# The 32nd largest of two sorted lists by a scan of maxima and minima, and the softmax division moved into the next step

## The chip, the cores and the metric

The kernel runs on one core of one Trainium2 chip. The metric is the device time of one launch, in microseconds (us). The kernel before took 1684.64 us, the median of three runs (1683.96 to 1685.89). The engines are called TensorE (PE; its weight loads PEld), VectorE (DVE), ScalarE (ACT), GpSimd (POOL) and SyncE (SP, which issues the DMA transfers here).

## The reference

Top-k attention, then a two-layer network with the SmeLU activation, all in fp32:

```python
# q, k, v: (B=8, H=8, S=576, D=64)
scores = scale * np.matmul(q, k.transpose(0, 1, 3, 2))
kth = np.partition(scores, -32, axis=-1)[..., -32:-31]
scores = np.where(scores >= kth, scores, -1000000000.0)
scores = scores - np.max(scores, axis=-1, keepdims=True)
attn = np.exp(scores)
attn = attn / (np.sum(attn, axis=-1, keepdims=True) + 1e-09)
attn_out = np.matmul(attn, v)
# (B,H,S,D) -> (B*S, H*D) = (4608, 512)
h = x @ w_in                                   # (512, 2048)
g = np.where(h >= 1, h, np.where(h <= -1, 0.0, (h + 1) ** 2 / 4.0))
out = g @ w_out                                # (2048, 512)
```

Each row of 576 scores keeps its 32 largest; what is kept is normalised by its sum plus 1e-9.

## The kernel before

The attention runs in 144 steps. A step handles 128 query rows of two heads, that is a tile of 128 partitions with 2 rows of 576 scores each, `s`. VectorE has an instruction that finds the 8 largest values of a row in falling order (`max`) and one that overwrites given 8 values in a row (`match_replace`). To make the rows half as long, the 576 scores are taken in 288 pairs: `more` holds the larger of each pair, `less` the smaller. The 32 largest of `more` come from four rounds, the 8 largest of `less` from one (`seconds`), and the 32nd largest of both lists together is the threshold `kth`. If more than 8 of the smaller ones could matter, `excess` shows it and a second, plain pass (`paired` is False) runs.

```python
def first_top(st):                      # of the next step, called within this one
    s = st["s"]
    if paired:
        pairs(st)                       # more = max of the two halves of s
    st["tops"] = tops = att.tile([P, 2, TOP_K + 8], F32, name="tops", bufs=3)
    st["e"] = e = att.tile([P, 2, S], F32, name="e", bufs=3)
    nmax = att.tile([P, 2], F32, name="nmax")
    for i in range(2):
        nc.vector.max(out=tops[:, i, 0:8], in_=(st["more"] if paired else s)[:, i, :])
    nc.scalar.activation(nmax, tops[:, :, 0], AF.Copy, scale=-1.0)
    for i in range(2):
        nc.scalar.activation(e[:, i, :], s[:, i, :], AF.Exp, bias=nmax[:, i:i + 1])
        yield

def weights(st, after):
    # ...
    for r in range(8, TOP_K, 8):
        for i in range(2):
            nc.vector.match_replace(out=rest[:, i, :], in_to_replace=tops[:, i, r - 8:r],
                                    in_values=src[:, i, :], imm_value=LOWEST)
        src = rest
        if r == 8:
            yield
        if r + 8 == TOP_K:
            yield
            yield from first_top(after) if after is not None else (None, None)
        for i in range(2):
            nc.vector.max(out=tops[:, i, r:r + 8], in_=src[:, i, :])
    if paired:
        nc.vector.tensor_tensor(out=less, in0=s[:, :, 0:SH], in1=s[:, :, SH:S], op=ALU.min)
        seconds = att.tile([P, 2, 8], F32, name="seconds")
        for i in range(2):
            nc.vector.max(out=seconds[:, i, :], in_=less[:, i, :])
        nc.vector.tensor_tensor(out=tops[:, :, TOP_K:TOP_K + 8], in0=tops[:, :, TOP_K - 2:TOP_K - 10:-1],
                                in1=seconds, op=ALU.min)
        for i in range(2):
            nc.vector.max(out=kth[:, i, :], in_=tops[:, i, TOP_K - 1:TOP_K + 8])
        last = kth[:, :, 0]
    # ...
    for i in range(2):                  # masks the exponentials, and sums them into z
        nc.vector.scalar_tensor_tensor(out=e[:, i, :], in0=s[:, i, :], scalar=last[:, i:i + 1],
                                       in1=e[:, i, :], op0=ALU.is_ge, op1=ALU.mult,
                                       accum_out=z[:, i:i + 1])
    yield
    rz = att.tile([P, 2], F32, name="rz")
    nc.vector.tensor_scalar(z, z, 1e-9, None, ALU.add)
    nc.vector.reciprocal(rz, z)
    if st["by_tensor"]:                 # the first 12 steps and the last 2
        # ... ScalarE scales an identity by rz; TensorE transposes and divides with it
    else:                               # the 130 others
        for i in range(2):
            nc.gpsimd.tensor_scalar(e[:, i, :], e[:, i, :], rz[:, i:i + 1], 1.0, ALU.mult, ALU.mult)
    # ... GpSimd notes the excess
    yield
```

In the 130 later steps the weights are transposed by DMA: ScalarE splits them into 16-bit halves, they go to DRAM, and a transposing DMA brings them back as `wT`, which `values` multiplies with v on TensorE.

```python
def move_w(st):
    # ...
    for i in range(2):
        nc.scalar.copy(halves[:, :, i * S:(i + 1) * S], st["e"][:, i, :].bitcast(U16).rearrange("p (k t) -> p t k", t=2))
    # ...
    nc.sync.dma_start(out=rows, in_=halves)
    nc.sync.dma_start_transpose(wT.bitcast(U16), rows.rearrange("p t k -> (p t) k"))
```

The two-layer network works on chunks of one or two tiles of 128 tokens. `hidden` makes 128 of the 2048 hidden values on TensorE (`ph`, 128 or 256 columns), ScalarE and GpSimd apply the activation, and `final` accumulates 512 outputs (`py`) on TensorE.

All engines are in order, and the order of their instructions is fixed when the program is built: a step has 7 slots, in each of which the attention's generator advances by one part and some units of the network are put in. How many is decided by a small model of the time, in which K_TIME stands for a step's length.

```python
K_TIME, PIECE_TIME, UNIT_TIME, SLOTS, EARLY_STEPS, EARLY_SHARE = 10.2, 0.55, 0.218, 7, 4, 32
# ...
for m in range(n + 2):
    # ...
        parts = [1] * SLOTS if early else [1, 1, 0, 1, 1, 1, 1]
    # ...
    for slot in range(SLOTS):
        # ...
        for _ in range(parts[slot]):
            next(top_k, None)
        # ...
        if slot == 2 and 1 <= m <= n and not state[m - 1]["by_tensor"]:
            move_w(state[m - 1])
            ready_at[m - 1] = done[m - 1] + 14.0
        # ...
        if slot == 4:
            begin_at(m + 2)             # the scores of the step after next
        if slot == 5 and not early:
            values_until(m - 1)
        # ...
        advance((EARLY_SHARE if early else share) / SLOTS if m < n else 32.0, now)
```

Of the kernel before, what the change touches and what calls it, by code (L numbers as in the profile page):

```python
# [10 lines left out]
F32 = mybir.dt.float32  # L11
# [3 lines left out]
AF = mybir.ActivationFunctionType  # L15
# [3 lines left out]
TOP_K = 32  # L19
# [5 lines left out]
def kernel(  # L25
# [37 lines left out]
    nc.gpsimd.memset(half, 0.5)  # L63
    minus = const.tile([P, 1], F32, name="minus")
    nc.gpsimd.memset(minus, -1.0)
    two = const.tile([P, 1], F32, name="two")
    nc.gpsimd.memset(two, 2.0)

# [9 lines left out]
    for i in range(2):  # L78
        v_tails.append([const.tile([P, H, D], F32, name=f"v_tail{i}{x}") for x in range(2)])
        for x in v_tails[i]:  # L80
            nc.gpsimd.memset(x, 0.0)

# [72 lines left out]
    def run(ctx, paired):  # L157
# [99 lines left out]
        def scores(st):  # L257
            t, hp, kT, qT = st["t"], st["hp"], st["keys"]["kT"], st["qT"]
            st["s"] = s = att.tile([P, 2, S], F32, name="s", bufs=3)
            for hf in range(2):  # L260
# [9 lines left out]
                                             start=True, stop=True)  # L270
                nc.scalar.activation(s[:, :, c0:c1], sp[:, :, 0:SH], AF.Copy, scale=SCALE)  # L271

# [6 lines left out]
        def first_top(st):  # L282
            s = st["s"]
            if paired:
                pairs(st)
            st["tops"] = tops = att.tile([P, 2, TOP_K + 8], F32, name="tops", bufs=3)
            st["e"] = e = att.tile([P, 2, S], F32, name="e", bufs=3)
            nmax = att.tile([P, 2], F32, name="nmax")
            for i in range(2):
                nc.vector.max(out=tops[:, i, 0:8], in_=(st["more"] if paired else s)[:, i, :])  # L290
            nc.scalar.activation(nmax, tops[:, :, 0], AF.Copy, scale=-1.0)
            for i in range(2):
                nc.scalar.activation(e[:, i, :], s[:, i, :], AF.Exp, bias=nmax[:, i:i + 1])  # L293
                yield


        def weights(st, after):
            s, m, tops, e = st["s"], st["m"], st["tops"], st["e"]
            kth = att.tile([P, 2, 8], F32, name="kth", bufs=3)
            if paired:  # L300
                src = rest = less = st["more"]
            else:
                src, rest = s, att.tile([P, 2, S], F32, name="rest", bufs=1)
            for r in range(8, TOP_K, 8):
                for i in range(2):
                    nc.vector.match_replace(out=rest[:, i, :], in_to_replace=tops[:, i, r - 8:r],  # L306
                                            in_values=src[:, i, :], imm_value=LOWEST)
                src = rest
                if r == 8:
                    yield  # L310
                if r + 8 == TOP_K:
                    yield
                    yield from first_top(after) if after is not None else (None, None)
                for i in range(2):
                    nc.vector.max(out=tops[:, i, r:r + 8], in_=src[:, i, :])  # L315
            if paired:
                nc.vector.tensor_tensor(out=less, in0=s[:, :, 0:SH], in1=s[:, :, SH:S], op=ALU.min)  # L317
                seconds = att.tile([P, 2, 8], F32, name="seconds")
                for i in range(2):
                    nc.vector.max(out=seconds[:, i, :], in_=less[:, i, :])  # L320
                nc.vector.tensor_tensor(out=tops[:, :, TOP_K:TOP_K + 8], in0=tops[:, :, TOP_K - 2:TOP_K - 10:-1],
                                        in1=seconds, op=ALU.min)
                for i in range(2):
                    nc.vector.max(out=kth[:, i, :], in_=tops[:, i, TOP_K - 1:TOP_K + 8])  # L324
                last = kth[:, :, 0]
            else:
                last = tops[:, :, TOP_K - 1]
            z = att.tile([P, 2], F32, name="z")
            for i in range(2):
                nc.vector.scalar_tensor_tensor(out=e[:, i, :], in0=s[:, i, :], scalar=last[:, i:i + 1],  # L330
                                               in1=e[:, i, :], op0=ALU.is_ge, op1=ALU.mult,
                                               accum_out=z[:, i:i + 1])
            yield
            rz = att.tile([P, 2], F32, name="rz")
            nc.vector.tensor_scalar(z, z, 1e-9, None, ALU.add)  # L335
            nc.vector.reciprocal(rz, z)  # L336
            if st["by_tensor"]:
                st["rz"] = diag = (late or words).tile([P, 2, P], F32, name="diag", bufs=1)
                for i in range(2):
                    nc.scalar.activation(diag[:, i, :], ident, AF.Copy, scale=rz[:, i:i + 1])  # L340
            else:
                for i in range(2):
                    nc.gpsimd.tensor_scalar(e[:, i, :], e[:, i, :], rz[:, i:i + 1], 1.0, ALU.mult, ALU.mult)  # L343
            if paired:
                nc.gpsimd.tensor_tensor(out=excess[:, 2 * m:2 * m + 2], in0=seconds[:, :, 7], in1=kth[:, :, 0],
                                        op=ALU.subtract)
            yield

# [112 lines left out]
        for b in range(0, B, 2):  # L463
            a, c, tl = [(b, t) for t in range(NT)], [(b + 1, t) for t in range(NT)], (b, NT)
            if b + 2 < B:
                rounds += a + [tl] + c + [(b + 1, NT)]
                chunks += [a[0:2], a[2:4], c[0:2], c[2:4], [tl]] if b else [[x] for x in a + c + [tl]]
            else:
                rounds += a + [tl, (b + 1, NT)] + c
                chunks += [a[0:2], a[2:4], [tl]] + [[x] for x in c]  # L470
        steps = []
        for b, t in rounds:
            tile_of = (b, t) if t < NT else (b - b % 2, t)
# [36 lines left out]
                inspected += 1  # L510


        K_TIME, PIECE_TIME, UNIT_TIME, SLOTS, EARLY_STEPS, EARLY_SHARE = 10.2, 0.55, 0.218, 7, 4, 32
        pe_time, dve_time, done, scored, ready_at, usable = 9.0, 12.0, {}, {}, {}, {0: 0.0}

        def advance(amount, until):
# [95 lines left out]
        for m in range(n + 2):  # L612
# [7 lines left out]
            top_k, parts = None, [0] * SLOTS  # L620
            if m < n:
                top_k = weights(state[m], state[m + 1] if m + 1 < n else None)
                parts = [1] * SLOTS if early else [1, 1, 0, 1, 1, 1, 1]
                start = max(dve_time, scored[m])
                now_converting = range(SLOTS) if m < EARLY_STEPS else range(0, SLOTS, 2)
                dve_time = start + K_TIME + PIECE_TIME * min(len(now_converting), n_pieces - converted)
                done[m] = dve_time
                state[m]["by_tensor"] = early or m >= n - 2
            for slot in range(SLOTS):
                now = start + (dve_time - start) * (slot + 1) / SLOTS  # L630
                for _ in range(parts[slot]):
# [9 lines left out]
                if slot == 1 and 1 <= m <= n and state[m - 1]["by_tensor"]:  # L641
                    pe_time = max(pe_time, done[m - 1] + 2.0) + 1.0
                    transpose_w(state[m - 1])
                    ready_at[m - 1] = pe_time + 1.8
                if slot == 2 and 1 <= m <= n and not state[m - 1]["by_tensor"]:
                    move_w(state[m - 1])
                    ready_at[m - 1] = done[m - 1] + 14.0
                if slot == 2 and m == n and paired:
                    judge(ps, att)
                if slot == 2 and (early or m == first_late or m >= n - 1):  # L650
# [71 lines left out]
```

## Time and profile before

| What | Value |
|---|---|
| median time | 1684.64 us |
| profiled span | 1683.5 us |
| TensorE busy, mean granted clock | 1549.2 us (92%), 0.952 |
| VectorE busy | 1550.5 us (92%) |
| ScalarE busy | 1188.2 us (71%) |
| GpSimd busy | 974.8 us (58%) |
| DMA engines, share of the span | 49.4% |

Busy shares are averages over the whole span. The first 200 us or so convert the weights beside the first attention steps; then come the later attention steps with the network beside them, until about 1608 us; then the network alone. A line of instructions in the profile gives the source line, the engine, the operation, the tiles written and read, the shapes and the count, then the busy time in us, the mean length of one in ns, and the idle time of the engine just before them. A line of waits gives who waited for whom, the total in us, how often, and the longest. In the slices, each digit is the busy share of a fortieth of the span in tenths.

### The profile page before, as it was taken

The page shows a single profiled execution, that of the slowest core. Times are in us where ns is not written, and L with a number is a line of the kernel's source. Part 1 is how long each engine was busy: PE and PEld are TensorE (multiplying, and loading weights), DVE is VectorE, ACT ScalarE, POOL GpSimd, SP SyncE. Part 2 cuts the span into 40 slices and gives each one's busy share as a digit, 9 for nine tenths or more (in the row PEclk, how much of TensorE's full clock was granted, in tenths as well). Part 3 has the DMA queues.
Part 4 walks back from the last instruction along what each step waited for, and adds up shares of the span by engine and source line. Part 5 has one row for each costly group of instructions (what it writes and reads, how often), then busy time and mean ns, then how long its engine had stood idle before and what let it go on. Part 6 is the DMA issues. An engine that isn't in the chain of part 4 may idle for free.

```text
span 1683.5 us, 30910 instructions
## 1 busy us (share of the span) xinstructions
PE 1549.2 (92%) x9645; PEld 1050.8 (62%) x9645; DVE 1550.5 (92%) x4875; ACT 1188.2 (71%) x2552; POOL 974.8 (58%) x1720
## 2 busy tenths in 40 slices
PE   5586999999998899979999999979999999999998
PEld 4464666666665666646566766646566666666675
DVE  6999999999999999999999999999999999999922
ACT  5677677777777767777677877767667877767743
POOL 4675677666665554536465755526465765657750
PEclk6698999999998999979999999979999999999999
DMA  9333345455555546554555555554555544544400
GB/s 246 114 98 91 86 132 160 129 151 141 140 154 156 144 135 174 142 157 135 146 159 143 150 142 151 158 158 124 155 150 151 143 131 130 132 133 117 114 27 16
DMA packets 439055, 227.83 MB, mean 135 GB/s; under 512 B 393056, under 2 KB 401248, under 8 KB 438880
## 3 DMA queue, kind: packets, MB, share of 16 engines
q1 hardware_dynamic: 438880, 225.75, 49.4%
q8 instruction: 78, 1.28, 0.3%
q14 instruction: 97, 0.79, 0.2%
HBM read 62.91 MB, written 86.11 MB: 89 GB/s over the span
## 4 chain that ended last, share of the span: by engine, by line
DVE 51%; PE 33%; ACT 7%; issue 3%; POOL 3%; DMA 2%; SPq 1%; DVEq 0%; POOLq 0%; ACTq 0%
PE ph L419 13%; DVE more L306 12%; PE py L444 12%; DVE tops L315 10%; DVE e L330 8%; DVE more L317 4%; DVE seconds L320 4%; DVE tops L290 4%; DVE more L279 4%; PE po L389 3%; PE sp L269 3%; ACT halves L372 2%; ACT e L293 1%; DVE z L335 1%; DVE kth L324 1%
## 5 line engine op out<-in xcount | busy, mean ns | idle before, releaser
L419 PEld LDWEIGHTS ph<-xT,w_in 128*128 128x128 f32 x3328 | 505.1, 195 | 199.0 <-issue 88.5
L419 PE MATMUL ph<-xT,w_in 128*128 128x128 f32 (+1 forms) x3328 | 594.1, 326 | 32.8 <-ACT g L431 18.6
L444 PE MATMUL py<-w_out,g 128*128 128x512 f32 x1152 | 564.3, 605 | 2.0 <-POOL w_out L136 1.8
L423 ACT ACTIVATE r<-ph,half 128x128 f32<-128x128 f32 (+1 forms) x416 | 169.7, 408 | 292.9 <-PE ph L419 237.6
L306 DVE MATCH_REPLACE8 more<-tops,more 128x288 f32<-128x288 f32 x864 | 375.6, 442 | 0.0
L436 POOL TENSOR_SCALAR r<-r 128x128 f32<-128x128 f32 (+1 forms) x392 | 164.9, 421 | 343.4 <-ACT r L423 342.1
L315 DVE MAX8 tops<-more 128x8 f32<-128x288 f32 x864 | 348.9, 445 | 0.0
L343 POOL TENSOR_SCALAR e<-e,rz 128x576 f32<-128x576 f32 x260 | 211.9, 825 | 205.2 <-DVE rz L336 205.2
L372 ACT COPY halves<-e 128x1152 uint16<-128x1152 uint16 x260 | 286.9, 1156 | 14.7 <-POOL e L343 14.0
L444 PEld LDWEIGHTS py<-w_out,g 128*128 128x128 f32 x1152 | 197.4, 191 | 145.9 <-issue 117.8
L438 POOL TENSOR_TENSOR g<-r,g 128x128 f32<-128x128 f32 (+1 forms) x400 | 261.6, 654 | 31.4
L330 DVE SCALAR_TENSOR_TENSOR e<-s,kth,e 128x576 f32<-128x576 f32 x288 | 242.0, 877 | 0.5
L437 POOL TENSOR_TENSOR r<-r 128x128 f32<-128x128 f32 (+1 forms) x392 | 219.0, 559 | 32.7
L293 ACT ACTIVATE e<-s,nmax 128x576 f32<-128x576 f32 x288 | 218.4, 771 | 4.8
L269 PE MATMUL sp<-kT,qT 64*128 64x288 f32 x1024 | 169.0, 447 | 9.9 <-ACT kT L229 9.1
L271 ACT ACTIVATE s<-sp 128x576 f32<-128x576 f32 x288 | 170.0, 642 | 6.6 <-PE sp L269 6.4
L389 PE MATMUL po<-wT,v_in 128*64 128x128 f32 x2048 | 148.5, 287 | 22.1 <-DMA wT<-rows 13.9
L389 PEld LDWEIGHTS po<-wT,v_in 128*64 128x64 f32 x2048 | 115.5, 141 | 80.7 <-issue 18.3
L431 ACT ACTIVATE g<-ph,minus 128x128 f32<-128x128 f32 (+1 forms) x400 | 162.4, 406 | 0.0
L269 PEld LDWEIGHTS sp<-kT,qT 64*128 64x128 f32 x1024 | 91.8, 193 | 84.6 <-issue 40.6
L320 DVE MAX8 seconds<-more 128x8 f32<-128x288 f32 x288 | 118.3, 452 | 13.9
L317 DVE TENSOR_TENSOR more<-s 128x576 f32<-128x576 f32 x144 | 122.4, 850 | 4.9
(88 smaller groups left out, 1349.6 us busy)
## 6 DMA issues: line engine op xcount, KB each, us to landing
rows<-halves SPq DMA_DIRECT2D x130, 576.0 KB, 2.8
raw<-in_moe_w_out_dram SPq DMA_DIRECT2D x52, 256.0 KB, 3.0
raw<-in_moe_w_in_dram SPq DMA_DIRECT2D x48, 256.0 KB, 3.1
k_in<-in_k_dram SPq DMA_DIRECT2D x64, 128.0 KB, 2.9
q_in<-in_q_dram SPq DMA_DIRECT2D x32, 256.0 KB, 3.1
v_in<-in_v_dram SPq DMA_DIRECT2D x8, 1024.0 KB, 6.0
out_dram<-y SPq DMA_DIRECT2D x32, 256.0 KB, 2.6
kT<-in_moe_w_in_dram SPq DMA_DIRECT2D x16, 256.0 KB, 4.5
```

The costliest lines, as they stand in the source:

```text
L269: nc.tensor.matmul(o[:, a0 - c0:a1 - c0], qT[d, g, :], kT[d, g, k0:k0 + a1 - a0], start=True, stop=True)
L293: nc.scalar.activation(e[:, i, :], s[:, i, :], AF.Exp, bias=nmax[:, i:i + 1])
L306: nc.vector.match_replace(out=rest[:, i, :], in_to_replace=tops[:, i, r - 8:r], in_values=src[:, i, :], imm_value=LOWEST)
L315: nc.vector.max(out=tops[:, i, r:r + 8], in_=src[:, i, :])
L330: nc.vector.scalar_tensor_tensor(out=e[:, i, :], in0=s[:, i, :], scalar=last[:, i:i + 1], in1=e[:, i, :], op0=ALU.is_ge, op1=ALU.mult, acc ...
L343: nc.gpsimd.tensor_scalar(e[:, i, :], e[:, i, :], rz[:, i:i + 1], 1.0, ALU.mult, ALU.mult)
L372: nc.scalar.copy(halves[:, :, i * S:(i + 1) * S], st["e"][:, i, :].bitcast(U16).rearrange("p (k t) -> p t k", t=2))
L389: nc.tensor.matmul(po[j * D:(j + 1) * D], v_in[:, h, c, :] if c < NT else v_tl[0][:, h, :], wT[:, block(j, c)], start=(c == 0), stop=(c == ...
L419: nc.tensor.matmul(ph, w_in[:, kk, f * P:(f + 1) * P], xT[:, kk, c0:c1], start=(kk == 0), stop=(kk == NK - 1))
L437: nc.gpsimd.tensor_tensor(out=r, in0=r, in1=r, op=ALU.mult)
L438: nc.gpsimd.tensor_tensor(out=g, in0=r, in1=g, op=ALU.add)
L444: nc.tensor.matmul(pys[i], gs[f][:, i * P:(i + 1) * P], w_out[:, f, :], start=(f == 0), stop=(f == NF - 1))
```

## The change

The step's short instructions between the last maximum and the masking are replaced by one scan. The sorted values of both rows now lie in one tile so that the second halves of the two lists are neighbours; the seconds lie, in reverse, beside them in a tile that is filled once with very large and very low values as separators. The scan keeps a running value: the maximum with the next of `tops`, then the minimum with the next of `seconds`. Position 8 gives the threshold of one row and position 24 that of the other.

The epsilon 1e-9 is added by ScalarE instead of VectorE in the 130 steps that transpose by DMA. It does so at the start of the next step (slot 0); reciprocal and division follow in that step's slot 1, and the copies for the DMA transpose in slot 3 in place of slot 2. The aim is to take short, dependent instructions off VectorE without letting it wait for what replaces them. The generator's parts are spread over all seven slots, K_TIME becomes 10.4, and in the last two batches all chunks are single tiles.

```diff
+    small = const.tile([P, 1], F32, name="small")
+    nc.gpsimd.memset(small, 1e-9)
 ...
+    SPLIT = TOP_K // 2
+    LAST = SPLIT + 8
+    second_lists = [const.tile([P, LAST + 1], F32, name=f"seconds{i}") for i in range(2)]
+    for x in second_lists:
+        nc.gpsimd.memset(x, LOWEST)
+        for i in range(2):
+            nc.gpsimd.memset(x[:, i * SPLIT:i * SPLIT + 1], LARGEST)
 ...
+        def eight(tops, i, r):
+
+            c = (r // SPLIT * 2 + i) * SPLIT + r % SPLIT
+            return tops[:, c:c + 8]
 ...
-            st["tops"] = tops = att.tile([P, 2, TOP_K + 8], F32, name="tops", bufs=3)
+            st["tops"] = tops = att.tile([P, 2 * TOP_K], F32, name="tops", bufs=3)
 ...
-                if r == 8:
+                if r + 8 < TOP_K:
                     yield
-                if r + 8 == TOP_K:
+                else:
                     yield
                     yield from first_top(after) if after is not None else (None, None)
 ...
-                seconds = att.tile([P, 2, 8], F32, name="seconds")
+                seconds = second_lists[m % 2]
                 for i in range(2):
-                    nc.vector.max(out=seconds[:, i, :], in_=less[:, i, :])
-                nc.vector.tensor_tensor(out=tops[:, :, TOP_K:TOP_K + 8], in0=tops[:, :, TOP_K - 2:TOP_K - 10:-1],
-                                        in1=seconds, op=ALU.min)
-                for i in range(2):
-                    nc.vector.max(out=kth[:, i, :], in_=tops[:, i, TOP_K - 1:TOP_K + 8])
-                last = kth[:, :, 0]
+                    nc.vector.max(out=seconds[:, (1 - i) * SPLIT + 1:(1 - i) * SPLIT + 9], in_=less[:, i, :])
+
+                nc.vector.tensor_tensor_scan(out=kth, data0=tops[:, 2 * TOP_K - 1 - LAST:2 * TOP_K], data1=seconds[:, LAST::-1],
+                                             initial=LOWEST, op0=ALU.max, op1=ALU.min)
+                last = [kth[:, 8:9], kth[:, LAST:LAST + 1]]
 ...
             yield
-            rz = att.tile([P, 2], F32, name="rz")
-            nc.vector.tensor_scalar(z, z, 1e-9, None, ALU.add)
-            nc.vector.reciprocal(rz, z)
             if st["by_tensor"]:
+                nc.vector.tensor_scalar(z, z, 1e-9, None, ALU.add)
+                rz = att.tile([P, 2], F32, name="rz")
+                nc.vector.reciprocal(rz, z)
 ...
-            else:
-                for i in range(2):
-                    nc.gpsimd.tensor_scalar(e[:, i, :], e[:, i, :], rz[:, i:i + 1], 1.0, ALU.mult, ALU.mult)
 ...
+        def add_to_sum(st):
+            nc.scalar.activation(st["z"], st["z"], AF.Identity, bias=small)
+
+        def divide(st):
+            rz = att.tile([P, 2], F32, name="rz")
+            nc.vector.reciprocal(rz, st["z"])
+            for i in range(2):
+                nc.gpsimd.tensor_scalar(st["e"][:, i, :], st["e"][:, i, :], rz[:, i:i + 1], 1.0, ALU.mult, ALU.mult)
+            note_excess(st)
 ...
-                chunks += [a[0:2], a[2:4], [tl]] + [[x] for x in c]
+                chunks += [[x] for x in a + [tl] + c]
 ...
-        K_TIME, PIECE_TIME, UNIT_TIME, SLOTS, EARLY_STEPS, EARLY_SHARE = 10.2, 0.55, 0.218, 7, 4, 32
+        K_TIME, PIECE_TIME, UNIT_TIME, SLOTS, EARLY_STEPS, EARLY_SHARE = 10.4, 0.55, 0.218, 7, 4, 32
 ...
-                parts = [1] * SLOTS if early else [1, 1, 0, 1, 1, 1, 1]
+                parts = [1] * SLOTS
 ...
+                if slot == 0 and moved:
+                    add_to_sum(state[m - 1])
+                if slot == 1 and moved:
+                    divide(state[m - 1])
-                if slot == 2 and 1 <= m <= n and not state[m - 1]["by_tensor"]:
+                if slot == 3 and moved:
                     move_w(state[m - 1])
-                    ready_at[m - 1] = done[m - 1] + 14.0
+                    ready_at[m - 1] = done[m - 1] + 15.0
```

(`moved` is the condition that stood in the line for slot 2; the note of the excess moves with the division.)

## The prediction

> **What bounds the kernel now.** I began with the page: busy shares, the slices of the span, the chain that ended last.
>
> ```profile
> span 1683.5 us, 30910 instructions
> ...
> PE 1549.2 (92%) x9645; PEld 1050.8 (62%) x9645; DVE 1550.5 (92%) x4875; ACT 1188.2 (71%) x2552; POOL 974.8 (58%) x1720
> ...
> PE   5586999999998899979999999979999999999998
> ...
> DVE  6999999999999999999999999999999999999922
> ```
>
> TensorE and VectorE are both busy for 92% of the span, in different places. VectorE is full from the second slice until it runs out of attention steps at about 1608 us; TensorE is short of work in the first four slices (weights are converted there) and still has 76 us to do at the end. The chain gives VectorE 51% and TensorE 33%. So neither bounds alone, and I asked for stretches of 100 us in the steady part, 210 to 1608 us (columns: length, then busy time of PE, PEld, DVE, ACT, POOL, granted clock, DMA).
>
> ```profile
> 710.00:810.00 100.00, 88.03 (x481) 56.57 (x481) 96.98 (x310) 69.16 (x133) 45.52 (x70) 0.88 0.51 139
> 910.00:1010.00 100.00, 99.28 (x615) 68.54 (x614) 96.83 (x307) 77.43 (x165) 65.00 (x116) 1.00 0.56 149
> 1310.00:1410.00 100.00, 100.00 (x595) 65.79 (x596) 97.05 (x305) 75.83 (x153) 60.29 (x102) 1.00 0.49 133
> ```
>
> VectorE stands at 95 to 97% everywhere: its idle 3% are the gaps between dependent instructions, and its waits on other engines in this part are 9.6 us in all. It sets the pace, a step each 10.75 us (mean of the steps from 430 us on, from the timeline). TensorE has 12 us to spare in one stretch and none in another. A faster VectorE pays only where TensorE has room. The fourteen stretches leave TensorE idle for 2.3, 7.1, 5.6, 8.9, 3.6, 12.0, 4.1, 0.7, 2.6, 8.9, 4.9, 0.0, 3.4 and (98 us long) 2.0 us, 66 us together.
>
> Next, the instructions concerned, in VectorE's groups with shapes kept apart, and the end of one step in the timeline (start, length in us).
>
> ```profile
> L324 DVE MAX8 kth<-tops 128x8 f32<-128x9 f32 x288 | 34.6, 162 | 5.0
> L335 DVE TENSOR_SCALAR z<-z 128x2 f32<-128x2 f32 x144 | 32.7, 227 | 4.6
> L321 DVE TENSOR_TENSOR tops<-tops,seconds 128x16 f32<-128x16 f32 x144 | 32.6, 226 | 4.9
> L336 DVE RECIPROCAL rz<-z 128x2 f32<-128x2 f32 x144 | 23.9, 166 | 4.9
> ```
>
> ```profile
> 905.78 0.17 DVE L321 TENSOR_TENSOR tops<-tops,seconds 128x16 f32<-128x16 f32 x1
> 905.99 0.24 DVE L324 MAX8 kth<-tops 128x8 f32<-128x9 f32 x2
> 906.19 0.82 DVE L330 SCALAR_TENSOR_TENSOR e<-s,kth,e 128x576 f32<-128x576 f32 x1
> ...
> 907.67 0.08 DVE L330 DVE_READ_ACCUMULATOR e<-s,kth,e 128x1 f32 x1
> 907.79 0.17 DVE L335 TENSOR_SCALAR z<-z 128x2 f32<-128x2 f32 x1
> 908.00 0.17 DVE L336 RECIPROCAL rz<-z 128x2 f32<-128x2 f32 x1
> 908.08 0.07 DVE L306 MATCH_VALUE_LOAD more<-tops,more 128x8 f32 x1
> ```
>
> These work on 2 to 16 elements and still cost about 0.17 us each, plus some 0.034 us of gap where one needs the result of the one before. They lie back to back on the engine that sets the pace, so their whole length counts. Over the late steps, from the end of the last seconds maximum to the start of the masking instruction (L330) takes 0.50 us on average, and from the end of its accumulator read to the first instruction of the next step 0.385 us.
>
> **What the Trainium skill says.** (1) "DVE: opcode table, instruction layouts, handler registers and perf-mode slots", Datapath and trigger behaviour: the scan of two tensors feeds its result back to an earlier stage and runs at half throughput. No run so far shows a scan. With the 0.96 GHz of "VectorE: DVE Perf Modes", Specifications, 25 elements at two cycles are 52 ns, an estimate. (2) "ScalarE: Activation LUTs", What ACT_TABLE_LOAD costs: an activation with immediates takes 186 ns plus 0.833 per element, a pointer operand 93 ns more. The trace has 209 ns for the 2-element nmax (page: 188), so the new addition with its bias tile should be about 0.3 us, an estimate. The trace has one table load in the whole run though Identity is used already, so none is added. (3) "TensorE: Matmul & The Clock Gate", Part 1: an idle TensorE falls to a lower clock. The trace agrees in kind: 0.88 where it was 88% busy, 1.00 where it was full. Filling idle time therefore also shortens the matmuls a little.
>
> **The change, part by part.**
> *The scan* removes the elementwise minimum and two small maxima in each of the 144 steps (0.50 us from seconds to masking) and puts one scan in: about 0.165 us fixed (the reciprocal's length for 2 elements) plus 0.05, and two gaps of 0.034, say 0.30. Saved: 0.20 us a step.
> *The epsilon* leaves VectorE in the 130 steps whose weights go through the DMA transpose. The 0.385 us at the step's end disappear altogether; the reciprocal comes back after the second match-replace of the next step, at 0.1 (overlapped, as now) to 0.2 us. Saved: 0.23 us in the middle. Together 0.43 us in 130 steps, 56 us, and 0.20 us in the 14 others, 3 us: 59 us of VectorE time. A late step goes from 10.75 to 10.32 us, which is 4.0 us per stretch of 100.
> *ScalarE* gets 130 additions of 0.3 us, 39 us at 71% busy: room enough.
> *What TensorE lets through.* In each stretch the gain is the smaller of 4.0 us and TensorE's idle time: seven stretches give 4.0, the others 2.3, 3.6, 0.7, 2.6, 0.0, 3.4 and 2.0; sum 42.6 us. With the 3 us of the early steps, 45.6 us.
> *Single chunks.* Of the last two batches, four token tiles are now multiplied one by one. The 256-column hidden matmul takes 316.1/1280 = 0.247 us, the 128-column one 278.0/2048 = 0.136; at 128 records a tile or a pair that is 17.4 us against 15.8 per tile, 1.6 us dearer, 6.4 us for four, on the engine that is full there. In return work is at hand four steps sooner; I give that no number.
> *The new wait.* VectorE's reciprocal now waits for ScalarE. From the trace I took how far ScalarE is behind: its copies in slot 2 (L372) start 2.8 us on average after VectorE has done the second match-replace (median 2.3, one in ten over 6.4). The addition is queued two slots earlier, some 2 to 3 us of ScalarE's time. So in the present timing it would come too late in perhaps four steps of ten, by 1 to 3 us. VectorE loses a rise of the lag once, not in each step, and much of it where TensorE is the bound anyway: 8 us.
> *Clock.* TensorE's busy time in the steady part is 1332 us at a mean clock of about 0.97; if a third of its idle time goes, some 5 us come back.
> Sum: 1684.6 - 45.6 + 6.4 + 8 - 5 = 1648.4, put as 1648 us.
>
> **The rivals.** *First: coupling eats it.* Today VectorE touches ScalarE's results only through scores made six slots ahead and exponentials; after the change it needs a sum that passed through ScalarE under 3 us before. If VectorE is held by its lag in most steps, by 0.3 us each, 40 us go and the time stays at 1680 to 1690. For it speaks the lag just quoted; against it that ScalarE is only 71% busy and that nearly all its idle time is waiting for TensorE.
>
> ```profile
> POOL e L343 <- DVE rz L336: 205.2, 45, 8.8
> ...
> ACT nmax L291 <- DVE tops L290: 46.9, 35, 2.9
> ```
>
> *Second: GpSimd is set free.* It waits 205 us for the reciprocal (45 times, 4.6 us each), and the hidden activations stand behind. If moving the division ends this, TensorE's waits on ScalarE (17 us for psum of the hidden layer) shrink too and VectorE's whole 59 us count: 1625 us. Against it: the division moves two slots down in GpSimd's order, and the reciprocal comes about 2.9 us later, two slots as well; I expect the wait to move and not to go.
> *Third: TensorE is the bound already.* Then only the 6.4 us of the singles show: 1690. The stretches with 7 to 12 us idle speak against it. *Fourth: the transposed weights come late.* Copies to DRAM start one slot, 1.5 us, later; TensorE waits for that DMA 13.9 us in all today, and could wait 10 us more.
>
> **Range and chances.** VectorE's saving alone, nothing else in the way, gives 1625; 1620 is the low end. Full coupling and a late transpose give 1690, the high end. The 2% lines are 1651 and 1718; my centre lies just under the first, so faster is about even, 0.50; within 2% 0.41; over 1718 needs waits larger than all that is saved, 0.09.
>
> **What would show it.** Right: a scan of about 0.21 us in 144 records; VectorE's busy time down by about 55 us; late steps near 10.4 us; TensorE's busy share up to 94%; a new wait of the reciprocal on ScalarE's z of 5 to 20 us; GpSimd's wait for the reciprocal still 150 us or more. Wrong: a scan over 0.4 us; the wait on z above 40 us; VectorE's idle time up by as much as its busy time fell; or TensorE idle over 66 us in the steady part although VectorE is faster.

## The result and the profile after

The changed kernel takes 1762.28 us (median; 1759.45 to 1763.67) against 1684.39 us before: ratio 1.046, 95% interval 1.044 to 1.048. It is slower by 78 us where the prediction had it faster by 36, and it lies 72 us above the high end of 1690 us.

The page of the kernel after (busy time and share by engine; the slices; the shares of the chain that ended last):

```profile
span 1760.7 us, 31335 instructions
...
PE 1565.0 (89%) x9901; PEld 1066.3 (61%) x9901; DVE 1508.8 (86%) x4457; ACT 1229.0 (70%) x2746; POOL 1012.9 (58%) x1823
...
PE   5687998899887898969899999969899999999998
...
DVE  6999877888879888998889998998989888888842
...
PE 53%; ACT 19%; DVE 16%; issue 4%; DMA 3%; POOL 3%; SPq 0%; POOLq 0%; ACTq 0%; DVEq 0%
```

The last of these lines, of the kernel before:

```profile
DVE 51%; PE 33%; ACT 7%; issue 3%; POOL 3%; DMA 2%; SPq 1%; DVEq 0%; POOLq 0%; ACTq 0%
```

VectorE was relieved as meant: 1550.5 us became 1508.8. But its slices, all nines before, are now sevens to nines, and in the chain its share falls from 51% to 16% while ScalarE's rises from 7% to 19%. The same three stretches as before (columns: length, then PE, PEld, DVE, ACT, POOL busy, clock, DMA) show both pace-setting engines with less to do at once:

```profile
710.00:810.00 100.00, 82.31 (x452) 53.31 (x452) 91.08 (x275) 70.19 (x143) 45.21 (x69) 0.90 0.51 140
910.00:1010.00 100.00, 98.23 (x568) 64.72 (x566) 89.95 (x266) 75.31 (x169) 61.27 (x111) 1.00 0.51 138
1310.00:1410.00 100.00, 96.62 (x605) 64.99 (x603) 90.75 (x270) 76.79 (x174) 61.58 (x116) 1.00 0.52 136
```

TensorE did not fill its gaps, it got larger ones (88.0 to 82.3 us busy in the first stretch). The waits say where both engines stand (who waits for whom: us in total, times, longest):

```profile
DVE rz L372 <- ACT z L368: 143.3, 101, 5.9
ACT nmax L308 <- DVE tops L307: 100.9, 72, 3.7
POOL e L374 <- DVE rz L372: 97.3, 16, 8.4
...
PE po L417 <- DMA wT<-rows: 45.1, 16, 5.0
PE ph L447 <- ACT g L459: 40.5, 36, 3.5
```

The first line is new: the reciprocal waits for the sum from ScalarE in 101 of 130 steps. ScalarE waits for VectorE's maxima twice as long as before (46.9 us), TensorE three times as long for the transposed weights (13.9) and twice as long for ScalarE to empty its hidden tiles (18.6). Of the kernel before:

```profile
PE ph L419 <- ACT g L431: 18.6, 25, 1.8
...
PE po L389 <- DMA wT<-rows: 13.9, 7, 3.6
...
DVE more L279 <- ACT s L271: 10.7, 12, 2.1
```

The whole loss lies in the attention. VectorE ends its last masking at 1692.3 us in place of 1607.2, 85 us later: it is busy 42 us less up to there, but waits 135 us more (waits are idle times over 0.15 us; its shorter gaps fell by 8 us). A late step takes 11.37 us in place of 10.76. What TensorE does after that became shorter by 8 us. These figures are worked out from the timelines, and so are those on the end of the attention below.

One place where VectorE waits for the sum in the timeline of the kernel after (start, length; in brackets the idle time before it and what ended it):

```profile
923.42 0.47 ACT L451 ACTIVATE r<-ph,half 128x256 f32<-128x256 f32 x1 [0.94 <-PE ph L447]
...
923.79 0.47 ACT L459 ACTIVATE g<-ph,minus 128x256 f32<-128x256 f32 x1
...
924.15 0.29 ACT L368 ACTIVATE z<-z,small 128x2 f32<-128x2 f32 x1
...
924.48 0.17 DVE L372 RECIPROCAL rz<-z 128x2 f32<-128x2 f32 x1 [2.05 <-ACT z L368]
```

ScalarE waits for a hidden tile, works it off, and only then adds the epsilon, 0.3 us of work that VectorE stands idle for 2 us to get.

### The profile page after: what moved, and what is told of

Read it like the earlier page. It is cut to its first block, busy times and chain, and to the rows that moved or that the text cites. A ratio compares the mean times of both kernels' runs of the same rounds, so it can differ in the third digit from the quotient of the medians.

```text
span 1760.7 us, 31335 instructions
## 1 busy us (share of the span) xinstructions
PE 1565.0 (89%) x9901; PEld 1066.3 (61%) x9901; DVE 1508.8 (86%) x4457; ACT 1229.0 (70%) x2746; POOL 1012.9 (58%) x1823
## 4 chain that ended last, share of the span: by engine, by line
PE 53%; ACT 19%; DVE 16%; issue 4%; DMA 3%; POOL 3%; SPq 0%; POOLq 0%; ACTq 0%; DVEq 0%
PE ph L447 22%; PE py L472 18%; ACT halves L400 6%; PE po L417 6%; PE sp L281 4%; DVE more L323 4%; ACT e L310 3%; DVE tops L332 3%; DMA wT<-rows 3%; ACT s L283 2%; ACT r L451 2%; DVE tops L307 2%; DVE more L296 2%; DVE e L346 2%; ACT g L459 2%
## 5 line engine op out<-in xcount | busy, mean ns | idle before, releaser
L447 PEld LDWEIGHTS ph<-xT,w_in 128*128 128x128 f32 x3584 | 523.7, 196 | 231.4 <-issue 88.5
L447 PE MATMUL ph<-xT,w_in 128*128 128x128 f32 (+1 forms) x3584 | 606.8, 317 | 59.2 <-ACT g L459 40.5
L464 POOL TENSOR_SCALAR r<-r 128x128 f32<-128x128 f32 (+1 forms) x424 | 152.9, 361 | 493.0 <-ACT r L451 491.6
L451 ACT ACTIVATE r<-ph,half 128x128 f32<-128x128 f32 (+1 forms) x448 | 178.4, 398 | 299.7 <-PE ph L447 253.9
L374 POOL TENSOR_SCALAR e<-e,rz 128x576 f32<-128x576 f32 x260 | 231.9, 903 | 97.3 <-DVE rz L372 97.3
L465 POOL TENSOR_TENSOR r<-r 128x128 f32<-128x128 f32 (+1 forms) x424 | 224.6, 530 | 35.3
L346 DVE SCALAR_TENSOR_TENSOR e<-s,kth,e 128x576 f32<-128x576 f32 x288 | 238.5, 865 | 6.0
L459 ACT ACTIVATE g<-ph,minus 128x128 f32<-128x128 f32 (+1 forms) x432 | 170.4, 394 | 0.0
L372 DVE RECIPROCAL rz<-z 128x2 f32<-128x2 f32 x130 | 21.3, 164 | 143.5 <-ACT z L368 143.3
L334 DVE TENSOR_TENSOR more<-s 128x576 f32<-128x576 f32 x144 | 132.8, 922 | 4.9
```

The source lines that it names most:

```text
L374: nc.gpsimd.tensor_scalar(st["e"][:, i, :], st["e"][:, i, :], rz[:, i:i + 1], 1.0, ALU.mult, ALU.mult)
L447: nc.tensor.matmul(ph, w_in[:, kk, f * P:(f + 1) * P], xT[:, kk, c0:c1], start=(kk == 0), stop=(kk == NK - 1))
L465: nc.gpsimd.tensor_tensor(out=r, in0=r, in1=r, op=ALU.mult)
```

## The experiments

Theories: **ring** (the sum's way over ScalarE closes a ring of waits between VectorE and ScalarE that is longer than a step), **blocked ScalarE** (first named for the run with the copies in slot 5: too much stands together in slot 3 of ScalarE's order, so it is late for the others), and as rivals the **constants** (K_TIME, single chunks), the **late path** of the weights through the transpose, and the **division's** place. The kernel before, run beside them, took 1683.2 to 1684.4 us in each group of runs.

TensorE's idle time below is worked out from the timelines: the gaps over 0.2 us between 210 and 1600 us, summed. It was 65 us before and is 123 us after.

### The scan alone

```diff
 (the kernel before, with the tiles, the scan and `last` of the diff; nothing else)
```

> The kernel before with the scan alone. Ring theory (the sum's way over ScalarE closes a ring of waits between VectorE and ScalarE that is longer than a step): no such ring here; the stretch from the last seconds maximum to the masking falls from 0.50 to 0.37 us, 144 times 0.13 is 18 us, so 1660 to 1672 us. Rival (the scan itself, or what it does to the engines' timing, is to blame): above 1700 us.

Measured: 1675.1 us, ratio 0.9945 (0.9926 to 0.9964). The scan is a gain, but 8 us and not 18: VectorE's busy time fell by 14 us, its waits rose by 3 us, and its attention ended 9.8 us earlier.

### The epsilon on VectorE, in the new slot

```diff
-                if slot == 0 and moved:
-                    add_to_sum(state[m - 1])
+            nc.vector.tensor_scalar(st["z"], st["z"], 1e-9, None, ALU.add)   # in divide, ahead of the reciprocal
```

> The kernel after, with the epsilon added by VectorE just ahead of the reciprocal in slot 1; slots, K_TIME and chunks as in after. Ring theory: the reciprocal waits for nothing, VectorE's idle time falls by some 140 us while its busy time rises by 30, late steps of about 10.7 us, 1665 to 1690 us. Rival (the new slots, K_TIME and single chunks cost the time): 1740 us or more.

Measured: 1731.1 us, ratio 1.029 (1.026 to 1.031). This lies between the two expected ranges: 31 us come back, 47 remain. It is not the dependency alone that changes here: VectorE's busy time rises by 49 us, where 30 were expected.

### The sum added by ScalarE, but read by nobody

```diff
-            nc.scalar.activation(st["z"], st["z"], AF.Identity, bias=small)
+            unread = att.tile([P, 2], F32, name="unread")
+            nc.scalar.activation(unread, st["z"], AF.Identity, bias=small)
```

> The kernel after, but ScalarE writes the sum with its epsilon into a tile that nobody reads, and the reciprocal takes the sum without the epsilon: the same ScalarE work, no wait for it. Ring theory: late steps near 10.4 us, 1635 to 1665 us. Rival (the 130 additions and their waits load ScalarE, which lies between TensorE and GpSimd): within 15 us of the 1762 us.

This kernel leaves the 1e-9 out of the division. Measured: 1720.3 us, ratio 1.022 (1.019 to 1.024). The 130 additions are all still there, so it is the dependency and not the work that costs 42 us. Both waits between the two engines go together: the reciprocal's of 143 us, and three quarters of ScalarE's wait for VectorE's maxima, 100.9 us in after. But 36 us over the kernel before remain. VectorE now waits elsewhere for the same engine (scores that ScalarE hands over):

```profile
DVE more L296 <- ACT s L283: 82.0, 56, 5.1
...
ACT nmax L308 <- DVE tops L307: 24.2, 21, 3.1
```

It had waited 10.7 us for them before. ScalarE is late also where VectorE does not wait for the sum: it finishes the unread addition 3.4 us after VectorE's second match-replace on average, and after it in 127 of 130 steps (from the timeline).

### The old constants

```diff
-EARLY_SHARE = 10.4, ...      chunks += [[x] for x in a + [tl] + c]
+EARLY_SHARE = 10.2, ...      chunks += [a[0:2], a[2:4], [tl]] + [[x] for x in c]
```

(The first number is K_TIME.)

> The kernel after with the old K_TIME 10.2 and the paired chunks of the last two batches. Ring theory: the ring stays, 1745 to 1765 us, lower by the 6 us of the dearer single chunks at most, with the reciprocal's wait on ScalarE still over 110 us. Rival (the retuned schedule is to blame): below 1720 us.

Measured: 1751.5 us, ratio 1.041 (1.038 to 1.043); the reciprocal still waits 132 us. The constants cost 11 us here.

### Copies back in slot 2

```diff
-                if slot == 3 and moved:
+                if slot == 2 and moved:
                     move_w(state[m - 1])
```

> The kernel after with ScalarE's copies for the DMA transpose back in slot 2; the division stays in slot 1. Ring theory: the 2.2 us of copies leave ScalarE's stretch between the maxima's negation in slot 3 and the sum in the next slot 0, the ring becomes shorter by up to 2 us, the reciprocal's wait on ScalarE falls below 100 us, and the copies end earlier, so the wait for the transposed weights falls as well: 1715 to 1740 us. Rival (the copies in slot 2 then wait for GpSimd's division, which comes too late for them): 1755 us or more, with over 60 us of that wait.

Measured: 1737.8 us, ratio 1.032 (1.030 to 1.034): the time fits the ring theory, the wait does not. The reciprocal's wait stays at 126 us, and ScalarE's copies now wait 144 us for GpSimd's division, as the rival had it. TensorE's wait for the transposed weights fell to 19 us in the steady part.

### No epsilon at all, old slots

```diff
 (scan alone, and)
-            nc.vector.tensor_scalar(z, z, 1e-9, None, ALU.add)
```

> The kernel before with the scan and without the addition of the epsilon at all (the sum holds exp(0) = 1 of the row's maximum, so 1e-9 changes no fp32 sum); reciprocal and division at the end of the step as before, old constants. VectorE loses 0.13 us of each step by the scan and some 0.24 by the addition, 50 us in all; TensorE lets through part of it: 1640 to 1660 us. Rival (TensorE has become the bound with the scan alone): within 6 us of the 1675.

This kernel leaves out the addition of 1e-9. Measured: 1665.4 us, ratio 0.990 (0.988 to 0.991); TensorE's idle time 56 us. The time lies between the two expected ranges. Of 38 us less VectorE time 18 arrive; VectorE's wait for scores from ScalarE rises from 10.7 us to

```profile
DVE more L287 <- ACT s L279: 34.3, 32, 2.8
```

This is the base for most of the kernels that follow. They leave the epsilon out as well, except where the text says "the kernel before" or "the kernel after".

### The new slots alone

> Scan, no epsilon and no addition on ScalarE, old K_TIME and chunks, but reciprocal and division in slot 1 of the next step and the copies in slot 3 as in after. If the late path of the weights (division, copies, transpose, product with v) costs what the unread sum left over, 1695 to 1715 us, with TensorE's wait for the transposed weights at 30 us or more. If the new constants cost it, 1660 us or less.

(Scan, no epsilon in the late steps; division in slot 1, copies in slot 3, the generator's parts and the 15.0 of `ready_at` as in the diff; old constants.) Measured: 1710.0 us, ratio 1.016 (1.014 to 1.017), with 33 us of TensorE's wait for the transposed weights. So the new slots cost 44.6 us without any wait for the sum. The late path was the theory at this point.

### The new constants alone

> Scan, no epsilon, old slots, but K_TIME 10.4 and single chunks in the last two batches. If the constants are the lesser part: 5 to 15 us above the same kernel with the old constants, so 1650 to 1675 us. If they are the greater: above 1690 us.

Measured: 1684.8 us, ratio 1.001 (1.000 to 1.002): 19.4 us, between the two expected ranges. TensorE's hidden matmuls became longer by 4.3 us only (591.5 to 595.8), so most of this is the schedule; K_TIME and the single chunks were not told apart.

### The copies alone in slot 3

```diff
-                if slot == 2 and 1 <= m <= n and not state[m - 1]["by_tensor"]:
+                if slot == 3 and 1 <= m <= n and state[m - 1] is not None and not state[m - 1]["by_tensor"]:
                     move_w(state[m - 1])
```

> Scan, no epsilon, division at the end of its own step as before, old constants, but the copies in slot 3 as in after. If the copies' later place alone costs most of the 45 us between the old and the new slots: 1690 us or more. If the division's place does: below 1680 us.

Measured: 1709.5 us, ratio 1.016 (1.014 to 1.017). One slot for two copies costs 44.1 us, about all that both new slots cost together. VectorE's attention ends 43.1 us later: it waits 30 us longer for the scores that ScalarE hands over (34.3 us became 64.6), and its own instructions take 11 us more. TensorE's idle time rises from 56 to 89 us, and of it the part that lies beside ScalarE's copies from 9.6 to 31.5 us. Waits of VectorE and TensorE, in the order of the listing:

```profile
DVE more L287 <- ACT s L279: 64.6, 39, 4.6
PE ph L430 <- ACT g L442: 37.6, 40, 3.8
PE po L400 <- DMA wT<-rows: 33.4, 16, 4.6
```

### The division alone in slot 1

> Scan, no epsilon, division in slot 1 of the next step as in after, old constants, but the copies in slot 2 as before. If the copies' place costs most: below 1685 us. If the division's place does: 1695 us or more, with ScalarE's copies waiting over 80 us for GpSimd's division.

(As the new slots alone, copies in slot 2.) Measured: 1730.2 us, ratio 1.029 (1.027 to 1.031), the copies waiting 173 us for GpSimd. With the division so late, slot 2 is worse for the copies than slot 3: once the division was moved, the copies had to move too, and slot 3 is a bad place as well.

### The products one step later

```diff
-                    values_until(m - 1)        # and wT with bufs=2, raw with bufs=2
+                    values_until(m - 2)        # and wT with bufs=3, raw with bufs=1
```

> The kernel with the new slots alone (scan, no epsilon, division in slot 1 of the next step, copies in slot 3, old constants; 1710 us), with the products of weights and v one whole step later and a third buffer for the transposed weights. If the late path of the weights holds TensorE and through it the scores: TensorE's wait for the transposed weights falls from 33 us below 8, VectorE's wait for scores from 62 below 35, 1670 to 1690 us. If the order on ScalarE and GpSimd is what costs: within 8 us of 1710.

Measured, on the new slots alone: 1705.0 us, ratio 1.013 (1.011 to 1.015). In the steady part the wait for the transposed weights is gone, and the same time stands in other lines; the two largest are

```profile
PE ph L447 <- ACT g L459: 38.9, 30, 3.3
PE pk L237 <- ACT s L283: 20.1, 4, 6.8
```

Nearly all of TensorE's waits there are for ScalarE now, and its idle time is 90 us (92 without the edit).

> Scan, no epsilon, old slots and constants (1665 us), with the products one whole step later and a third buffer for the transposed weights. Here the transposed weights are waited for by 15.5 us only, so the late path theory gives 1650 to 1662 us; the rival theory, by which TensorE's order does not matter, gives 1665 us.

Measured, on the old slots without epsilon: 1674.3 us, ratio 0.994 (0.992 to 0.995), 9 us worse than without the edit, which neither theory expected. In both kernels the later products leave TensorE more to do after the attention: 78.0 us became 87.5 there, 76.8 became 89.2 here. So the edit has a cost of its own. If that cost is the same 9 us in both, taking the wait off was worth 14 us of the 44.6 (5.0 and 8.9 together), an estimate. The late path is a part of the loss, then, and not the main one.

### The copies in slot 5

```diff
 (new slots alone, products one step later, and)
-                if slot == 3 and moved:
+                if slot == 5 and moved:
                     move_w(state[m - 1])
```

> As the kernel with the products one step later (scan, no epsilon, division in slot 1 of the next step, three buffers for the transposed weights; 1705 us), but ScalarE's copies in slot 5 in place of slot 3. Blocked-ScalarE theory (2.2 us of copies behind the exponential and ahead of the scores keep ScalarE too long from emptying TensorE's hidden tiles): slot 5 has room, TensorE's idle time in the steady part falls from 90 to below 65 us, 1665 to 1685 us. Rival (the division's later place costs it through GpSimd): 1700 us or more.

Measured: 1688.4 us, ratio 1.003 (1.002 to 1.004): 17 us come back with the division still late, which speaks against the division as the main cause; the time is 3 us above the range of the blocked-ScalarE theory. TensorE's idle time is 77 us, less of a fall than expected, and the part beside the copies rose from 28 to 43 us. What fell is TensorE's wait for ScalarE to empty its hidden tiles, in the steady part from 38.9 us to

```profile
PE ph L447 <- ACT g L459: 7.2, 11, 1.2
```

and VectorE's wait for scores, from 47.8 to 31.1 us. In return TensorE waits longer for the copies of the attention's output (`xT`, 16.9 us became 32.2).

### The sign check out of slot 3

ScalarE also checks the signs of the weights, 1.4 us in slot 3 of every other step. One edit in four kernels:

```diff
-                elif slot == 3 and late is not None:
+                elif slot == 6 and late is not None:
                     if m % 2:
                         inspect()
```

> As the kernel with the copies alone in slot 3 (1709.5 us), but the check of the weights' signs, 1.4 us of ScalarE in slot 3 of every other step, put into slot 6. Blocked-ScalarE theory: slot 3 becomes lighter by 0.7 us on average and a part of the 44 us comes back, 1685 to 1702 us. Rival (not the length of the block but the copies' own lateness): within 5 us of 1709.

Measured, with the copies alone in slot 3: 1685.9 us, ratio 1.001 (1.000 to 1.002): 23.6 us come back.

> Scan, no epsilon, old slots and constants (1665 us), with the check of the signs in slot 6 in place of slot 3. Blocked-ScalarE theory: TensorE idles less beside the sign checks (7.5 us of its idle time lies beside them), 1655 to 1664 us. Rival: 1665 us or more.

Measured, with the scan, no epsilon, old slots: 1649.6 us, ratio 0.980 (0.978 to 0.981), the best version here; 15.8 us gained, more than expected.

> The kernel before with one edit: the check of the signs in slot 6 in place of slot 3. If VectorE's shortened step is what made the best version fast and the sign check only lets it through, VectorE still sets the pace here with its 10.75 us steps: 1676 to 1685 us. If ScalarE's block was the bound already: 1670 us or less.

Measured, on the kernel before: 1669.3 us, ratio 0.991 (0.989 to 0.993): 15 us from this edit alone. VectorE's wait for scores, 10.7 us, falls to 0.4, and its attention ends 12.6 us earlier. ScalarE's slot 3 was holding the kernel back already before the change. So the two parts of the best version are worth about 15 and 20 us, and VectorE's shorter step is needed for the second.

> The kernel after with the sign check in slot 6 in place of slot 3. Blocked-ScalarE theory: slot 3, in which after puts the copies too, becomes lighter by 0.7 us on average; 15 to 30 us come back as in the kernel with the copies alone in slot 3, 1732 to 1748 us, with the reciprocal's wait on ScalarE below 130 us. Ring theory, by which the sum's way from slot 3 to the next slot 0 holds as much ScalarE work as before (slot 6 lies on it too): within 8 us of 1762, the wait unchanged.

Measured, on the kernel after: 1731.2 us, ratio 1.029 (1.027 to 1.031): 31 us come back, 1 us more than the blocked-ScalarE theory allowed. The reciprocal still waits 123.8 us for the sum, and ScalarE waits longer for the maxima (114.0 us).

The edit is worth 15 to 16 us where slot 3 holds no copies and 24 to 31 us where it does, as a crowded slot would have it. Crowding is not all, though: with the check out of the way the copies in slot 3 still cost 36 us (1649.6 against 1685.9). Each without the other, both cost about in proportion to their length: the checks are 91 us of ScalarE's time in all and cost 15 to 16 us, the copies are 285 us and cost 36.

### The division one slot later still

```diff
-                if slot == 1 and moved:
+                if slot == 2 and moved:
                     divide(state[m - 1])
```

> The kernel after with the reciprocal and the division one slot later, in slot 2; the sum stays in slot 0, the copies in slot 3. Ring theory: ScalarE gets 1.6 us more between sum and reciprocal and VectorE's part of the ring shrinks by as much, so the reciprocal's wait on ScalarE falls from 143 to below 70 us; the copies may wait for GpSimd instead, 1730 to 1755 us. Rival (the wait only shows that ScalarE is behind, and moves along with the reciprocal): the wait, with what VectorE then waits for scores, stays above 110 us, 1755 us or more.

Measured: 1768.8 us, ratio 1.051 (1.048 to 1.053). Both waits between the two engines fell, and the time did not:

```profile
DVE rz L372 <- ACT z L368: 114.0, 74, 4.3
...
ACT nmax L308 <- DVE tops L307: 45.5, 39, 3.5
```

Against 143.3 and 100.9 us in after. The time and the wait are those of the rival, but the run does not decide between the theories, as it brings two new costs. ScalarE's copies now wait 57.7 us for GpSimd's division (5.6 in after), and the masking grew longer, as the division falls beside it more often (the last section has the measure):

```profile
L346 DVE SCALAR_TENSOR_TENSOR e<-s,kth,e 128x576 f32<-128x576 f32 x288 | 274.2, 987 | 6.0
```

In after it was 238.5 us, 865 ns each. VectorE's waits fell by 32 us and its busy time rose by 37.

What becomes of the ring: as the only cause it fell with the unread sum, where 36 us remain, and with the new slots alone, where no sum is waited for and 45 us are lost. For the other 42 us, those of the dependency, two engines that wait for each other are what the waits show. That they form a closed ring longer than a step is not shown.

### The account

| Step | Time, us | Difference |
|---|---|---|
| before | 1684.4 | |
| scan alone | 1675.1 | -9.3 |
| no epsilon | 1665.4 | -9.7 |
| copies to slot 3 | 1709.5 | +44.1 |
| division to slot 1 | 1710.0 | +0.5 |
| new constants, unread sum | 1720.3 | +10.3 |
| the reciprocal reads ScalarE's sum | 1762.3 | +42.0 |

The line "division to slot 1" also holds the generator's new parts and `ready_at`; the one below it also holds the work of ScalarE's additions. The order of the steps matters: in the old slots the constants alone cost 19.4, and the division alone, with the copies in slot 2, 65.

## Why the prediction was wrong

Set against the sum of the prediction, the account misses it by 114 us: 44 for the copies' slot, which the sum charged nothing, 34 for the new wait (42 in place of 8), 27 for the saving (19 in place of 45.6), 5 for the clock and 4 for the constants.

**What bounds the kernel.** Right that VectorE and TensorE share the pace and that VectorE's saving would pass only in part. Wrong was the step "in each stretch the gain is the smaller of 4.0 us and TensorE's idle time", 42.6 us. With no new wait at all (scan, no epsilon, old slots) it was 19 us. The idle time of TensorE is not free room: of the 65 us before, 51.5 were waits for ScalarE. And a faster VectorE runs into ScalarE as well: its wait for scores rose from 10.7 to 34.3 us. Moving 1.4 us of ScalarE's work gave 15 us where VectorE was not touched.

**The scan.** Right in size where GpSimd is idle: 0.211 us as estimated with the half throughput that the Trainium skill states ("DVE: opcode table, instruction layouts, handler registers and perf-mode slots", Datapath and trigger behaviour). The mean is larger, as the group's row shows (mean ns after the bar):

```profile
L339 DVE TENSOR_TENSOR_SCAN kth<-tops,seconds 128x25 f32<-128x25 f32 x144 | 43.2, 300 | 4.9
L372 DVE RECIPROCAL rz<-z 128x2 f32<-128x2 f32 x130 | 21.3, 164 | 143.5 <-ACT z L368 143.3
```

From the last seconds maximum to the masking 0.50 us became 0.37 on average, so 0.13 us a step were saved and not 0.20. VectorE's busy time fell by 42 us, not 55.

**ScalarE's addition.** 0.304 us each, 39.6 us in all, as estimated. "Room enough" was the error: 71% busy is an average, and what counted was what stands ahead of the addition in the order.

**The new wait.** This step failed in its mechanism: "VectorE loses a rise of the lag once, not in each step, and much of it where TensorE is the bound anyway: 8 us". Measured: 143 us of wait, 42 us of time. "Once" was wrong, because the wait comes back: ScalarE's slot 3 begins with the negated maximum, which waits for VectorE, and where VectorE is held up ScalarE is held up next (100.9 us, and 24.2 with the sum unread). The lag of 2.8 us was read rightly from the trace, but "too late in perhaps four steps of ten", inferred from it, did not carry over: the wait came in 101 of 130 steps. Why so often stays open. The crowded slot 3 alone is not the reason, as the wait is still 124 us without the sign check in it, and 126 us with the copies in slot 2, where they wait for GpSimd instead. The first rival named this wait and priced it at 0.3 us a step; it was 1.1.

**The copies' slot.** This step failed by the most: the sum charged the move nothing, and the fourth rival at most 10 us of waiting for the transpose. It cost 44 us, and for the greater part not that way: taking that wait off gave 5 us, some 14 with the edit's own cost set aside. The prediction did not look at what else is in slot 3 on ScalarE: the negated maximum, an exponential of 0.77 us, every other time 1.4 us of sign checks, and now 2.2 us of copies, while TensorE has two buffers for its hidden tiles and waits for ScalarE to empty them. Behind the copies stand the second exponential and the scores that VectorE waits for, as in this place of the kernel after:

```profile
1171.08 0.20 ACT L308 ACTIVATE nmax<-tops 128x2 f32<-128x2 f32 x1 [2.00 <-DVE tops L307]
1171.31 0.78 ACT L310 ACTIVATE e<-s,nmax 128x576 f32<-128x576 f32 x1
...
1171.99 2.19 ACT L400 COPY halves<-e 128x1152 uint16<-128x1152 uint16 x2
...
1174.09 0.77 ACT L310 ACTIVATE e<-s,nmax 128x576 f32<-128x576 f32 x1
...
1174.89 1.19 ACT L283 ACTIVATE s<-sp 128x576 f32<-128x576 f32 x2
```

**The constants.** Single chunks were charged 6.4 us, K_TIME nothing. Together they cost 11 to 19 us.

**The clock.** The 5 us rested on TensorE's idle time going. It rose from 65 to 123 us, and the mean granted clock of the run went from 0.952 to 0.948.

**GpSimd.** The wait for the reciprocal was expected to stay at 150 us or more; it fell to 97. The time did not gain by it; TensorE's waits for GpSimd in the steady part were under 1 us in after.

What stays open: the way from ScalarE's slot 3 to the 44 us was not followed link by link. Shown is that the time follows what is put in that slot: the copies in, their move on to slot 5, and the sign check out in four kernels. On VectorE's side most of the loss is waiting for scores. On TensorE's side 22 of the 33 us of added idle time lie beside the copies when they alone are moved, but only 20 of 58 us between before and after. How much is the length of the block, and how much that it stands ahead of the scores, was not told apart.

## What to carry to other kernels

Moving a short instruction from the busiest engine to one with time to spare pays only if nobody has to wait for its result soon: price the dependency by where the other engine stands in its order at that moment, not by its busy share. In a schedule fixed in advance, look at how much each engine has in each slot before moving work by a slot; two copies put one slot later on an engine that is 71% busy cost 44 us here, more than the 42 us of VectorE's time that the change saved. And try the parts apart: the scan was worth keeping, and dropping an addition that changes no fp32 value did what the move was meant to do.

## What the hardware showed

Here VectorE's instructions that read two tensors grow longer when GpSimd works beside them; the maxima, which read one, do not. In after, the scan takes 0.211 us with GpSimd idle (66 of them) and 0.423 us when GpSimd is busy for over 90% of it (31); the masking 0.816 and 0.987 us; the 8 largest of a row 0.445 and 0.446 us. With the new slots alone, where the late division falls beside the masking, this is 1.121 us (180 of 288), and VectorE's busy time was 19 us above that with the old slots. With the division one slot later still it is 1.113 us (148 of 288, where after has 61). The Trainium skill says that such an instruction and a GpSimd instruction that reads SBUF exclude each other ("SBUF — State Buffer", SBUF: two separate sides); the runs agree in which instructions are hit. The cost of moving work to GpSimd's busy hours thus appears on VectorE.
